# Linear attention and two feed-forward layers on one core: additions moved from GpSimd to VectorE, token quarters loaded singly, order laid anew

## The chip, the core and the metric

The kernel runs on one core of a Trainium2 chip. The metric is device microseconds of one execution, the median of several runs. The core has TensorE (PE, matmuls into PSUM), VectorE (DVE), ScalarE (ACT), GpSimd (POOL), and SyncE (SP), whose queue issues nearly all DMAs. PEld is TensorE's weight load. Each engine works through its own queue in order, with semaphores between them.

## What is computed

Attention with positive features over 4 batches of 8 heads, 576 tokens, head size 64; then two feed-forward layers over the 2304 tokens of width 512, with 2048 inner features.

```python
def _attn_ref(q, k, v, w_phi):
    def phi(x):
        proj = np.einsum('bhsd,df->bhsf', x, w_phi)
        proj = proj - np.max(np.abs(proj), axis=-1, keepdims=True)
        return np.concatenate([np.exp(proj), np.exp(-proj)], axis=-1)
    q_p, k_p = (phi(q), phi(k))
    kv = np.einsum('bhsf,bhsd->bhfd', k_p, v)
    z = np.sum(k_p, axis=2)
    num = np.einsum('bhsf,bhfd->bhsd', q_p, kv)
    den = np.einsum('bhsf,bhf->bhs', q_p, z)[..., None] + 1e-06
    return (num / den).astype(np.float32)
# layer 1: h = x @ w_in; g = h / (1 + exp(-h)); x = g @ w_out
# layer 2: h = max(x @ w_in, 0); out = (h * h) @ w_out
```

## The kernel before

Matmuls of the layers keep nearly full float32 precision: every operand is split into a high part (a cast on ScalarE, `hi_act`, L495) and a low part (source minus high part, `lo_on`, L499), and a product is three matmuls.

The work runs in this order. In **attention**, two heads (a pair) make a unit. `keys_of` (L810) makes the feature sums of keys and values. `queries_of` (L963) takes half of a batch's 576 tokens twice: projection (L1001, L1002), copy out of PSUM on ScalarE (L1016), the largest magnitude over the 128 features, which lie on partitions, by `partition_all_reduce` on GpSimd (L1023), its subtraction on VectorE (L1029), two exponents on ScalarE (L1042), splits, products with the key sums (L1076), and a division through a round trip to HBM. GpSimd also writes ones into the value tiles by memsets (L831, L833).

Interleaved with it, **layer 1 for the first 1280 tokens** runs in plain form: four token blocks of 288, 288, 352 and 352 by 16 chunks of inner features (`chunk`, L1144; products L1161 and L1200). Weights come as 64-bit words and are converted (`w_conv`). `w1_store` (L657) adds each chunk's high and low parts together again and stores the result, for the next part; it makes two additions of 128x512 for each of 16 chunks.

**Layer 1 for the other 1024 tokens, and layer 2**, use a seven-product scheme (Strassen-Winograd) on 2x2 blocks, which needs sums of weight blocks and of token blocks. `w_sums` (L729) loads four 128x256 quarters, splits three of them, makes four sums in place (`w_adds`, L714) and splits those; there are eight pairs of chunks `q` in each of the layers A, B (layer 1, first and second matrix), C and D (layer 2), 32 sets in all. `y_ahead` (L761) does the same earlier for five sets of B and D and parks the result in HBM through the three shared `raw` buffers. `x_sums` (L1227) loads four quarters of a token block, makes four sums and seven splits: once for layer 1 (on VectorE), three times for layer 2. `quad` (L1310) makes the seven products of a first matrix (L1333), combining PSUM banks on VectorE (L1349). `fold` (L1397) loads the activations, makes sums (L1425, L1428, L1431), splits, and the products of a second matrix (L1478).

Order and buffers come from a planner in the kernel (`Plan`): every operation has an engine, an assumed cost, a key (due time) made from the table `KEYS` (L354), and the buffers it holds. At each point an engine takes the ready operation of lowest key, and the instructions are emitted in the order of these starts. Costs and keys thus decide the order in each engine's queue, but nothing on the chip is timed by them. A waiting instruction holds up everything behind it in its queue. A `fixed` buffer is a set place in memory, a `homed` one the next free buffer of a pool.

Of the kernel before, what the change touches and what calls it, by code (L numbers as in the profile page):

```python
# [54 lines left out]
XOWN = {0: (("g0", 0), ("g1", 0), ("g2", 0), ("fs", 0)), 1: (None, None, None, ("x0", 6144))}  # L55
# [291 lines left out]
def dma(kb):  # L347
# [18 lines left out]
def attention_then_two_mlps(ctx, tc, kT, qT, v, w_phi, w1, w2, out):  # L366
# [362 lines left out]
    def w_sums(layer, q, key):  # L729
# [26 lines left out]
        op(key, "POOL", 3700, lambda: w_adds(f), r=[(W, "lo", 0), (W, "lo", 1)], w=[(W, 1)], bufs=[f], unit=u)  # L756
# [4 lines left out]
    def y_ahead(layer, q, key):  # L761
# [5 lines left out]
        def piece(name, a, b, o, r):  # L767
            t = homed("raw", (128, 2, b - a, 256), F32R)
# [18 lines left out]
        gate = [(("ya", layer, AHEAD[layer][k - 1]), "d", "d")] if k else []  # L787
# [3 lines left out]
        op(key, "POOL", 3700, lambda: w_adds(f), r=[(Y, "a"), (Y, "b")], w=[(Y, 1)], bufs=[f], unit=u)  # L791
# [18 lines left out]
    def keys_of(j, p, key):  # L810
# [136 lines left out]
        op(key, "PE", 450, kv_end, r=[(K, "kv", 0), (K, "kv", 1), *done[2]], w=[(K, "t")], bufs=[ps, kv, vt, both], unit=u)  # L947
# [15 lines left out]
    def queries_of(b, p, key, lo_engine="DVE"):  # L963
# [97 lines left out]
        for a in range(2):  # L1061
# [22 lines left out]
            op(key, "PE", 970 if whole else 6 * MM, num_mm, r=[(K, "kvl"), (Q, el, 0), (Q, el, 1)], w=[(Q, "n", a)],  # L1084
# [142 lines left out]
    def x_sums(m, s, key):  # L1227
# [16 lines left out]
        keep = own if alone else own + new  # L1244
# [15 lines left out]
        op(key - 6, "SP", dma(4 * qb), load, r=deps, w=[(X, "raw")], bufs=own)  # L1260

        def split(prod, src, r, key=key, keep=keep):
# [10 lines left out]
            op(key, "ACT", act(2 * qb), hi, r=r, w=[(X, "hi", prod)], bufs=[*keep, b], unit=u)  # L1273
            op(key, "DVE", dve(2 * qb), lo, r=[*r, (X, "hi", prod)], w=[(X, "lo", prod)], bufs=[*keep, b], unit=u)
# [5 lines left out]
        def add(out, x, y, r, name):  # L1280
            e = "DVE" if m == 1 else "POOL"
# [12 lines left out]
        add(t1, b12, b11, first + after(1), "t1")
        add(t3, b22, b12, first + [(X, "t1")], "t3")
        add(t2, b22, t1, [(X, "t1"), (X, "t3")] + after(3), "t2")
        add(t4, b21, t2, [(X, "t2")] + after(2), "t4")
        split(6, t2, [(X, "t2")])
# [98 lines left out]
    def fold(m, i, q, key):  # L1397
# [9 lines left out]
        at_f = None if m == 1 and k < 3 else FOLD[m]["f"][k % 3]  # L1407
# [27 lines left out]
        def split(name, a, b, r):  # L1435
# [3 lines left out]
            engine = "POOL" if m == 1 and name == "a" else "DVE"  # L1439
# [178 lines left out]
    for k, q in enumerate(AHEAD["D"]):  # L1618
        at = base2 + NQ * step * P["ya"] + P["yb"] * k
# [85 lines left out]
```

## Time and profile before

| | us |
|---|---|
| median of 3 runs | 1054.42 |
| lowest, highest | 1051.50, 1059.72 |
| the profiled execution | 1062.31 |
| its span, first to last instruction | 1060.4 |

| engine | busy us | share of the span |
|---|---|---|
| TensorE matmul | 954.4 | 90% |
| VectorE | 762.2 | 72% |
| ScalarE | 610.6 | 58% |
| GpSimd | 278.0 | 26% |

The mean granted clock of TensorE is 0.956 of full speed. A share is an average over stretches with different limits: attention and plain layer 1 until about 519 us, products of `quad` for layer 1 until 590, `fold` until 704, `quad` for layer 2 until 871, and its `fold` to the end. A busy time of TensorE is modelled and is longer at the lower clock. In a table of groups, what follows the bar is busy time, the mean of one, then the idle time of the engine just before them with what ended it ("<-"). "issue" is time in which an engine waited for nothing that the profile shows.

### The profile page before, as it was taken

Reading aid. Unit: us, or ns where it says so; the run is one execution under the profiler, and the core shown is the slowest. Engines: PE = TensorE matmul, PEld = TensorE weight load, DVE = VectorE, ACT = ScalarE, POOL = GpSimd, SP = SyncE. Lnnn points to the kernel's source line nnn. Section 1 sums busy time; section 2 is a strip of 40 time slices with the busy share of each in tenths; the row PEclk is TensorE's granted clock in tenths of the full one; section 3 lists DMA queues with packets and bytes.
Section 4 is the critical chain, followed back from the end, with each engine's and each line's share of the span. In section 5 each row is a group of like instructions: output and inputs, shape, how many; then the busy total and the mean of one; then the engine's idle time right before and its main releaser. Section 6 shows DMA issues by size and latency. Waiting matters only on the chain.

```text
span 1060.4 us, 17832 instructions
## 1 busy us (share of the span) xinstructions
PE 954.4 (90%) x6454; PEld 899.9 (85%) x6454; DVE 762.2 (72%) x1251; ACT 610.6 (58%) x1298; POOL 278.0 (26%) x276
## 2 busy tenths in 40 slices
PE   8889999997676867898899969989999999999998
PEld 7579898897576867788788859989999999999998
DVE  6778988674476454775966799996766678988852
ACT  7777877784354564763654544456656565444431
POOL 2400221102344332343243272463230123000000
PEclk9899999998888978899999989999999999999999
DMA  7689758883466657568456854346463666545422
GB/s 227 216 270 334 258 164 252 267 283 137 152 214 198 216 170 229 173 190 249 139 218 229 277 200 146 114 150 235 150 241 126 234 239 226 162 123 154 140 80 81
DMA packets 103289, 208.45 MB, mean 197 GB/s; under 512 B 16288, under 2 KB 48416, under 8 KB 98080
## 3 DMA queue, kind: packets, MB, share of 16 engines
q1 hardware_dynamic: 103056, 207.23, 59.9%
q8 instruction: 51, 0.84, 0.3%
q14 instruction: 38, 0.31, 0.1%
q10 hardware_dynamic: 144, 0.07, 0.0%
HBM read 136.07 MB, written 71.11 MB: 195 GB/s over the span
## 4 chain that ended last, share of the span: by engine, by line
PE 43%; DVE 11%; issue 4%; DMA 3%; ACT 2%; POOL 2%; SPq 0%; DVEq 0%; POOLq 0%; ACTq 0%
PE y L1478 16%; PE pb L1333 10%; PE pc L1333 6%; PE pa L1333 6%; DVE RA L499 3%; PE h L1161 2%; PE o L1200 2%; DVE x L499 1%; DVE b_w L499 1%; DMA rd<-rr 1%; POOL b_raw L716 1%; DMA b_t<-rd 1%; PE pn L1076 1%; DVE FA L1425 1%; POOL b_t L1023 1%
## 5 line engine op out<-in xcount | busy, mean ns | idle before, releaser
L716 POOL TENSOR_TENSOR b_raw<-b_raw 128x256 f32<-128x256 f32 x128 | 114.6, 898 | 215.3 <-DVE b_w L499 57.9
L495 ACT CAST RA<-x 128x512 fp32r<-128x512 f32 (+2 forms) x146 | 82.4, 587 | 92.2 <-PE y L1478 51.7
L1478 PE MATMUL y<-RA,b_w 128*128 128x256 f32 x912 | 127.0, 281 | 1.6 <-DVE RA L499 1.1
L1478 PEld LDWEIGHTS y<-RA,b_w 128*128 128x128 f32 x912 | 115.7, 189 | 2.4 <-DVE RA L499 1.7
L499 DVE TENSOR_TENSOR RA<-x,RA 128x512 fp32r<-128x512 f32 (+2 forms) x146 | 92.4, 649 | 30.6 <-ACT RA L495 29.9
L1023 POOL PARTITION_ALL_REDUCE b_t<-b_t x28 | 63.2, 2284 | 159.2 <-ACT b_t L1016 66.6
L1478 PE MATMUL y<-RA,b_wq 128*128 128x256 f32 x600 | 90.5, 284 | 5.3 <-DVE RA L499 2.9
L1478 PEld LDWEIGHTS y<-RA,b_wq 128*128 128x128 f32 x600 | 81.9, 192 | 6.5 <-DVE RA L499 3.7
L1200 PE MATMUL o<-b_g,b_w 128*128 128x288 f32 (+1 forms) x420 | 76.6, 326 | 2.5 <-DVE b_g L499 2.5
L1029 DVE TENSOR_TENSOR b_t<-b_t,b_t 128x576 f32<-128x576 f32 x28 | 29.5, 1054 | 65.0 <-POOL b_t L1023 64.9
L1076 PE MATMUL pn<-b_t,b_kv 128*65 128x288 f32 x320 | 58.1, 330 | 18.4 <-ACT b_t L495 6.6
L1200 PE MATMUL o<-b_g,b_wq 128*128 128x352 f32 (+1 forms) x348 | 65.3, 329 | 8.7 <-DVE b_g L499 5.9
L1042 ACT ACTIVATE b_t<-b_t 128x576 f32<-128x576 f32 x56 | 37.7, 681 | 59.2 <-DVE b_t L1029 52.6
L1200 PEld LDWEIGHTS o<-b_g,b_w 128*128 128x128 f32 x420 | 67.1, 201 | 3.8 <-DVE b_g L499 3.5
L1161 PE MATMUL h<-b_x,b_w 128*128 128x288 f32 (+1 forms) x420 | 69.2, 315 | 1.1 <-DVE FA L1169 1.1
L1076 PEld LDWEIGHTS pn<-b_t,b_kv 128*65 128x65 f32 x320 | 43.5, 146 | 30.1 <-DVE b_kv L940 6.9
L1333 PE MATMUL pb<-RA,b_w 128*128 128x384 f32 (+1 forms) x312 | 68.8, 350 | 0.0
L1161 PEld LDWEIGHTS h<-b_x,b_w 128*128 128x128 f32 x420 | 64.9, 195 | 1.6 <-DVE FA L1169 1.4
L1200 PEld LDWEIGHTS o<-b_g,b_wq 128*128 128x128 f32 x348 | 56.5, 199 | 11.1 <-DVE b_g L499 7.0
L499 DVE TENSOR_TENSOR b_t<-b_t,b_t 128x576 fp32r<-128x576 f32 (+1 forms) x72 | 55.6, 780 | 12.0 <-ACT b_t L495 10.4
L1161 PE MATMUL h<-b_x,b_wq 128*128 128x352 f32 (+1 forms) x348 | 58.5, 319 | 1.8 <-DVE FA L1169 0.9
L499 DVE TENSOR_TENSOR b_w<-b_raw,b_w 128x1024 fp32r<-128x1024 f32 (+2 forms) x59 | 54.8, 939 | 6.6 <-ACT b_w L495 5.2
(188 smaller groups left out, 2243.0 us busy)
## 6 DMA issues: line engine op xcount, KB each, us to landing
b_wq<-w1d SPq DMA_DIRECT2D x18, 1024.0 KB, 7.2
b_raw<-w SPq DMA_DIRECT2D x32, 512.0 KB, 5.9
x<-gd SPq DMA_DIRECT2D x32, 512.0 KB, 3.7
gd<-g SPq DMA_DIRECT2D x36, 384.0 KB, 2.4
b_w<-w SPq DMA_DIRECT2D x11, 1024.0 KB, 7.5
w2d<-FA SPq DMA_DIRECT2D x32, 256.0 KB, 4.4
w1f<-b_raw SPq DMA_DIRECT2D x16, 512.0 KB, 3.2
b_raw<-w1f SPq DMA_DIRECT2D x32, 256.0 KB, 4.1
```

The source lines that it names most:

```text
L495: nc.scalar.copy(out=dst, in_=src)
L499: e.tensor_tensor(out=dst, in0=src, in1=hi.bitcast(F32), op=ALU.subtract)
L716: nc.gpsimd.tensor_tensor(out=get(f)[:, o], in0=get(f)[:, a], in1=get(f)[:, b], op=how)
L1023: nc.gpsimd.partition_all_reduce(get(mx), get(pr).rearrange("p a t -> p (a t)"), 128, bass.bass_isa.ReduceOp.absmax)
L1029: nc.vector.tensor_tensor(out=f, in0=f, in1=get(mx), op=ALU.subtract)
L1042: nc.scalar.activation(out=flat(e), in_=f, func=AF.Exp, scale=1.0 - 2.0 * s)
L1076: nc.tensor.matmul(get(ps)[:D1, :HB], w, flat(e)[:, t], start=x == 0, stop=x == len(ops) - 1)
L1161: nc.tensor.matmul(get(ps)[:, :cols], a, x[:, cc, :cols], start=k == 0, stop=k == 3 * ND - 1)
L1200: nc.tensor.matmul(get(acc)[:, :cols], a, g, start=c == 0 and x == 0, stop=c == NC - 1 and x == 2)
L1333: nc.tensor.matmul(get(ps)[:, :qb], ws[a][:, f], get(b)[:, y, cc], start=first and k == 0, stop=k == 5, skip_group_check=True,)
L1425: nc.vector.tensor_tensor(out=part(0, 2), in0=get(f)[:, 1:4:2, :half], in1=part(0, 2), op=ALU.subtract)
L1478: nc.tensor.matmul(get(acc)[:, d * 256:d * 256 + half], get(ws[a][0])[:, ws[a][1], s], both(y)[:, j], start=q == 0 and d == 0 and x == 0, ...
```

## The change

All four kinds of additions that GpSimd made go to VectorE: the four sums of a weight set (`w_adds`), the merges in `w1_store` (one of 128x1024 in place of two of 128x512), the token sums of layer 2 in `x_sums`, and the low part of split "a" in `fold` of layer 1. `x_sums` loads its four quarters as four operations, each with its own dependants and buffers, in place of one. The first inputs of layer 1's `fold` have other homes, as have the fourth quarter of layer 2's first token block and the pieces of `y_ahead` for D, which waits for the first product of layer 2. Some of the planner's costs change by a little, and the keys nearly all change.

```diff
-XOWN = {0: (("g0", 0), ("g1", 0), ("g2", 0), ("fs", 0)), 1: (None, None, None, ("x0", 6144))}
+XOWN = {0: (("g0", 0), ("g1", 0), ("g2", 0), None), 1: (None, None, None, ("x0", 6144))}
@@ FOLD
-    1: {"f": (("FA", 0), ("FA", 4096), None), ...
+    1: {"f": (("fs", 0), ("FA", 0), ("FA", 4096)), ...
@@ KEYS (the part that is named below; nearly all others change too)
-    "ss": 35.86, "wa": -0.61, "wb": 4.29, "wc": 32.0, "ba": 46.13, "bb": 9.59, "x1": 32.79, "x2": 28.35, "xe":
+    174.03, "ss": -10.38, "wa": -1.73, "wb": 9.37, "wc": 3.99, "ba": 32.07, "bb": 33.22, "x1": 114.67, "x2":
+    -3.46, "xe": 17.39, "mg": 6.56, "md": 524, "mp": 304, "me": 50,
@@ w1_store
-        def merge(x):
-            nc.gpsimd.tensor_tensor(out=get(f)[:, x], in0=halves(0)[:, x], in1=halves(1)[:, x], op=ALU.add)
+        def merge():
+            nc.vector.tensor_tensor(out=get(f), in0=halves(0), in1=halves(1), op=ALU.add)
...
-        u = plan.unit()
-        for x in range(2):
-            op(key, "POOL", pool(512), lambda x=x: merge(x), r=r + [(("c", 0, i, c), "h")], w=[("wm", c, x)], bufs=[w, f], unit=u)
-        op(key, "SP", dma(512), store, r=[("wm", c, x) for x in range(2)], w=[(("wf", 0, c), "d")], bufs=[f])
+        op(key, "DVE", dve(1024), merge, r=r + [(("c", 0, i, c), "h")], w=[("wm", c)], bufs=[w, f], unit=plan.unit())
+        op(key, "SP", dma(512), store, r=[("wm", c)], w=[(("wf", 0, c), "d")], bufs=[f])
@@ w_adds
-            nc.gpsimd.tensor_tensor(out=get(f)[:, o], in0=get(f)[:, a], in1=get(f)[:, b], op=how)
+            nc.vector.tensor_tensor(out=get(f)[:, o], in0=get(f)[:, a], in1=get(f)[:, b], op=how)
@@ w_sums
-        op(key, "POOL", 3700, lambda: w_adds(f), r=[(W, "lo", 0), (W, "lo", 1)], w=[(W, 1)], bufs=[f], unit=u)
+        op(key, "DVE", 4 * dve(256), lambda: w_adds(f), r=[(W, "lo", 0), (W, "lo", 1)], w=[(W, 1)], bufs=[f], unit=u)
@@ y_ahead
-            t = homed("raw", (128, 2, b - a, 256), F32R)
+            shape = (128, 2, b - a, 256)
+            t = homed("raw", shape, F32R) if layer == "B" else fixed(("RA", 43008 if b - a == 2 else 47104), shape, F32R)
...
-        gate = [(("ya", layer, AHEAD[layer][k - 1]), "d", "d")] if k else []
+        gate = [(("ya", layer, AHEAD[layer][k - 1]), "d", "d")] if k else [(("q", 2, 0, 0), "p1")] if layer == "D" else []
...
-        op(key, "POOL", 3700, lambda: w_adds(f), r=[(Y, "a"), (Y, "b")], w=[(Y, 1)], bufs=[f], unit=u)
+        op(key, "DVE", 4 * dve(256), lambda: w_adds(f), r=[(Y, "a"), (Y, "b")], w=[(Y, 1)], bufs=[f], unit=u)
@@ x_sums
-        def load():
-            for i in range(2):
-                for j in range(2):
-                    at = (2 * s + j) * qb
-                    nc.sync.dma_start(out=raw(i, j if i == 0 else 1 - j), in_=(x1d if m == 1 else x2d)[:, 2 * i:2 * i + 2, at:at + qb])
+        def load(i, j):
+            at = (2 * s + (j if i == 0 else 1 - j)) * qb
+            nc.sync.dma_start(out=raw(i, j), in_=(x1d if m == 1 else x2d)[:, 2 * i:2 * i + 2, at:at + qb])
...
-        op(key - 6, "SP", dma(4 * qb), load, r=deps, w=[(X, "raw")], bufs=own)
+        for i, j in ((0, 0), (0, 1), (1, 0), (1, 1)):
+            op(key - 6, "SP", dma(qb), lambda i=i, j=j: load(i, j), r=deps, w=[(X, "raw", i, j)], bufs=[ob(i, j)])
...
-        def add(out, x, y, r, name):
-            e = "DVE" if m == 1 else "POOL"
+        def add(out, x, y, r, name, keep):
+            e = "DVE"
@@ fold
-        at_f = None if m == 1 and k < 3 else FOLD[m]["f"][k % 3]
+        at_f = FOLD[m]["f"][k % 3] if m == 2 or k not in (1, 2) else None
...
-            engine = "POOL" if m == 1 and name == "a" else "DVE"
+            engine = "DVE"
```

## Rows read from the trace of the kernel before

**Rows 1.** Busy time by stretch: from:to, length, engines (instructions), clock, DMA share, GB/s.

```profile
75.00:219.00 144.00, 135.34 (x1045) 130.33 (x1044) 115.62 (x208) 112.38 (x267) 23.28 (x25) 0.99 0.83 263
219.00:460.00 241.00, 184.52 (x1193) 175.07 (x1193) 136.82 (x226) 131.47 (x343) 78.94 (x66) 0.87 0.60 192
460.00:519.00 59.00, 51.63 (x293) 47.77 (x292) 43.27 (x65) 32.22 (x60) 17.72 (x21) 0.97 0.75 226
...
590.00:704.00 114.00, 96.74 (x728) 91.86 (x726) 104.44 (x145) 55.31 (x99) 57.76 (x51) 0.96 0.55 180
704.00:871.00 167.00, 166.56 (x952) 166.18 (x953) 114.39 (x191) 104.29 (x205) 43.51 (x40) 1.00 0.56 200
```

**Rows 2.** Waits, 219 to 519 us: who waited for whom, us, times, longest.

```profile
DVE b_t L1029 <- POOL b_t L1023: 62.9, 9, 11.2
POOL b_t L1023 <- issue: 50.1, 7, 9.6
ACT b_t L1042 <- DVE b_t L1029: 49.9, 8, 10.9
```

**Rows 3.** Instructions of L1023, L663 and L716: count, ns min/median/max, first and last start.

```profile
L1023 POOLq MODIFY_POOL_CONFIG  x18: 1/11/40, 245.9 to 446.8; - x18
...
L663 POOLq MODIFY_POOL_CONFIG  x16: 87/98/98, 219.5 to 408.1; - x16
...
L716 POOLq MODIFY_POOL_CONFIG  x4: 4/46/88, 434.8 to 460.8; - x4
```

**Rows 4.** Timeline of GpSimd, 110 to 135 us: start, us, instruction, idle before.

```profile
121.62 2.14 POOL L1023 PARTITION_ALL_REDUCE b_t<-b_t  x1 [5.05 <-ACT b_t L1016]
```

**Rows 5.** Timeline of all engines, 251 to 258 us.

```profile
252.18 2.16 POOL L1023 PARTITION_ALL_REDUCE b_t<-b_t  x1 [6.45 <-issue]
254.37 0.76 DVE L1029 TENSOR_TENSOR b_t<-b_t,b_t 128x576 f32<-128x576 f32 x1 [7.63 <-POOL b_t L1023]
...
255.22 0.68 ACT L1042 ACTIVATE b_t<-b_t 128x576 f32<-128x576 f32 x1 [7.11 <-DVE b_t L1029]
...
256.24 0.61 PE L1001 MATMUL pq<-b_t,wst_lo 128*128 128x288 f32 x1 [6.67 <-ACT b_t L1016]
```

**Rows 6.** Timeline of TensorE, 219 to 470 us: the last of eight stalls.

```profile
429.73 2.71 PE L1200 MATMUL o<-b_g,b_wq 128*128 128x352 f32 x8 [4.86 <-DVE b_g L499]
```

**Rows 7.** VectorE by form, whole span: the L1115 and L1284 groups.

```profile
L1115 DVE TENSOR_TENSOR b_xx<-b_t,b_t 64x288 f32<-64x288 f32 x56 | 31.5, 563 | 7.5 <-DMA b_t<-rd 6.9
...
L1284 DVE TENSOR_TENSOR b_wl<-b_wl,b_wl 128x1024 f32<-128x1024 f32 x2 | 2.4, 1217 | 0.0
```

**Rows 8.** VectorE by form, 900 to 1050 us.

```profile
L499 DVE TENSOR_TENSOR RA<-x,RA 128x512 fp32r<-128x512 f32 x86 | 58.0, 687 | 29.2 <-ACT RA L495 28.8
...
L1428 DVE TENSOR_TENSOR x<-x 128x256 f32<-128x256 f32 x26 | 10.9, 419 | 0.1
```

**Rows 9.** VectorE by form, 590 to 704 us: first and last of 19 forms.

```profile
L499 DVE TENSOR_TENSOR x<-FA,x 128x512 fp32r<-128x512 f32 x17 | 16.7, 987 | 0.3 <-ACT x L495 0.2
...
L499 DVE TENSOR_TENSOR b_wl<-b_raw,b_wq 128x256 fp32r<-128x256 f32 x2 | 1.4, 682 | 0.0
```

**Rows 10.** GpSimd by form in 75 to 219, 219 to 460 and 590 to 704 us.

```profile
L1023 POOL PARTITION_ALL_REDUCE b_t<-b_t x10 | 22.7, 2293 | 80.3 <-ACT b_t L1016 42.8 <-DMA b_v<-v 19.9 <-issue 9.1
...
L1023 POOL PARTITION_ALL_REDUCE b_t<-b_t x15 | 32.4, 2182 | 77.5 <-issue 50.1 <-ACT b_t L1016 13.2 <-DMA rd<-rr 8.3
...
L716 POOL TENSOR_TENSOR b_raw<-b_raw 128x256 f32<-128x256 f32 x32 | 31.4, 982 | 16.5 <-DVE b_w L499 7.5 <-DMA b_w<-ysdB 4.5 <-DVE b_wl L499 2.2
```

**Rows 11.** Chain that ended last, 860 to 900 us: start, us, what.

```profile
883.16 2.69 POOL b_raw L716
...
887.89 0.75 POOL b_raw L716
```

**Rows 12.** Waits of GpSimd, 590 to 900 us.

```profile
POOL b_raw L716 <- DMA gd<-g: 46.3, 1, 46.3
...
POOL x L1284 <- DMA b_raw<-x2d: 25.9, 3, 13.1
```

More of the change, by code (lines that the diff above doesn't have):

```diff
@@ L860, in keys_of @@
         both = slot(f"kd{n}_2", u, (128, 2, F))
-        op(key, "PE", NKT * 218 + 140, proj, r=[(K, "raw"), "wraw"], w=[((K, a), "p") for a in range(2)],
+        op(key, "PE", NKT * 218 + 220, proj, r=[(K, "raw"), "wraw"], w=[((K, a), "p") for a in range(2)],
            bufs=[raw, *pk[:2], *mxs[:2]], unit=u)
-        op(key, "PE", 218, proj_end, r=[(K, "end"), "wraw", ((K, 0), "p")], w=[((K, 2), "p")], bufs=[end, pk[2], mxs[2]], unit=u)
+        op(key, "PE", 140, proj_end, r=[(K, "end"), "wraw", ((K, 0), "p")], w=[((K, 2), "p")], bufs=[end, pk[2], mxs[2]], unit=u)
         for g in range(3):
@@ L1009, in queries_of @@
         if whole:
-            op(key - (P["p1"] if b == 1 else 0), "PE", 4 * 120 + 140, proj_rows, r=[(Q, "raw"), "wraw"],
+            op(key - (P["p1"] if b == 1 else 0), "PE", 4 * 120 + 210, proj_rows, r=[(Q, "raw"), "wraw"],
                w=[(Q, "p", a) for a in range(2)], bufs=[raw, *pqs, pr], unit=u)
@@ L1083, in queries_of @@
             el = "e" if whole else "el"
-            op(key, "PE", 970 if whole else 6 * MM, num_mm, r=[(K, "kvl"), (Q, el, 0), (Q, el, 1)], w=[(Q, "n", a)],
+            op(key, "PE", 990 if whole else 6 * MM + 6, num_mm, r=[(K, "kvl"), (Q, el, 0), (Q, el, 1)], w=[(Q, "n", a)],
                bufs=[kv, ps, num] + [x for hl_ in hls for x in hl_], unit=u)
@@ L1243, in x_sums @@
             fresh = lambda i, j: get(new[2 * i + j])
-        keep = own if alone else own + new
-        def load():
-            for i in range(2):
-                for j in range(2):
-                    at = (2 * s + j) * qb
-                    nc.sync.dma_start(out=raw(i, j if i == 0 else 1 - j), in_=(x1d if m == 1 else x2d)[:, 2 * i:2 * i + 2, at:at + qb])
+        ob = lambda i, j: own[i] if m == 1 else own[2 * i + j]
+        nb = ob if alone else lambda i, j: new[2 * i + j]
+        def load(i, j):
+            at = (2 * s + (j if i == 0 else 1 - j)) * qb
+            nc.sync.dma_start(out=raw(i, j), in_=(x1d if m == 1 else x2d)[:, 2 * i:2 * i + 2, at:at + qb])
         if m == 1:
@@ L1259, in x_sums, with split @@
         turn = [(("xr", m, s - 1), "lo", prod) for prod in SLOT] if s else []
-        op(key - 6, "SP", dma(4 * qb), load, r=deps, w=[(X, "raw")], bufs=own)
-        def split(prod, src, r, key=key, keep=keep):
+        for i, j in ((0, 0), (0, 1), (1, 0), (1, 1)):
+            op(key - 6, "SP", dma(qb), lambda i=i, j=j: load(i, j), r=deps, w=[(X, "raw", i, j)], bufs=[ob(i, j)])
+        def split(prod, src, r, keep, key=key):
             b = fixed(XT[m][prod], (128, 2, 2, qb), F32R)
@@ L1272, in split @@
             r = [*r, *turn]
-            op(key, "ACT", act(2 * qb), hi, r=r, w=[(X, "hi", prod)], bufs=[*keep, b], unit=u)
-            op(key, "DVE", dve(2 * qb), lo, r=[*r, (X, "hi", prod)], w=[(X, "lo", prod)], bufs=[*keep, b], unit=u)
+            op(key, "ACT", act(2 * qb), hi, r=r, w=[(X, "hi", prod)], bufs=[keep, b], unit=u)
+            op(key, "DVE", dve(2 * qb), lo, r=[*r, (X, "hi", prod)], w=[(X, "lo", prod)], bufs=[keep, b], unit=u)
         b11, b12 = (lambda: raw(0, 0)), (lambda: raw(0, 1))
@@ L1288, in x_sums @@
-        first = [(X, "raw")]
+            op(key - 1, e, dve(2 * qb) if e == "DVE" else pool(2 * qb), go, r=r, w=[(X, name)], bufs=list(dict.fromkeys(keep)), unit=u)
+        r11, r12, r22, r21 = ((X, "raw", i, j) for i, j in ((0, 0), (0, 1), (1, 0), (1, 1)))
         after = (lambda *ps: [(X, "lo", p) for p in ps]) if alone else (lambda *ps: [])
-        split(1, b11, first)
+        split(1, b11, [r11], ob(0, 0))
         if alone:
-            split(2, b21, first)
-            split(3, b22, first)
@@ L1294, in x_sums @@
[L1294 to L1298, printed above, removed]
+            split(2, b21, [r21], ob(1, 1))
+            split(3, b22, [r22], ob(1, 0))
+        add(t1, b12, b11, [r11, r12] + after(1), "t1", [ob(0, 1), ob(0, 0), nb(0, 0)])
+        add(t3, b22, b12, [r12, r22, (X, "t1")], "t3", [ob(1, 0), ob(0, 1), nb(0, 1)])
@@ L1299, in x_sums @@
+        add(t2, b22, t1, [r22, (X, "t1"), (X, "t3")] + after(3), "t2", [ob(1, 0), nb(0, 0), nb(1, 0)])
+        add(t4, b21, t2, [r21, (X, "t2")] + after(2), "t4", [ob(1, 1), nb(1, 0), nb(1, 1)])
+        split(6, t2, [(X, "t2")], nb(1, 0))
         if not alone:
-            split(2, b21, first)
-        split(7, t3, [(X, "t3")])
-        split(5, t1, [(X, "t1")] + ([(X, "t2")] if alone else []))
+            split(2, b21, [r21], ob(1, 1))
+        split(7, t3, [(X, "t3")], nb(0, 1))
+        split(5, t1, [(X, "t1")] + ([(X, "t2")] if alone else []), nb(0, 0))
@@ L1303, in x_sums @@
         if not alone:
-            split(3, b22, first)
+            split(3, b22, [r22], ob(1, 0))
         if m == 2 and s == 0:
-            later.append(lambda key: split(4, t4, [(X, "t4")], key, own[3:]))
+            later.append(lambda key: split(4, t4, [(X, "t4")], nb(1, 1), key))
         else:
-            split(4, t4, [(X, "t4")])
+            split(4, t4, [(X, "t4")], nb(1, 1))
     def quad(m, s, q, key):
```

7 lines of the change are left out of this document (3 added, 4 removed), and 13 rows, old and new, of tables (FOLD, KEYS).

## The prediction

> **What bounds the kernel now.** The table by stretches comes first. From 704 to 871 us TensorE is busy 166.56 of 167 us and nothing is to be had there [rows 1]. Two long stretches are not full. In 219 to 460 TensorE idles 241 - 184.52 = 56.5 us and its granted clock is 0.87; in 75 to 219, the same mix of attention and first-layer chunks, it idles 8.7 of 144 at 0.99 [rows 1]. In 590 to 704 TensorE has 96.74 of 114, while VectorE has 104.44 of 114: VectorE bounds that stretch [rows 1].
>
> Then the waits of 219 to 519. The longest is a chain: VectorE's subtraction (L1029) waited 62.9 us for GpSimd's partition reduction (L1023), ScalarE's exponent (L1042) 49.9 us for that subtraction, and the reduction itself 50.1 us for "issue", that is for nothing the profile shows [rows 2]. The reader should ask what GpSimd does in those 50 us. The instructions of the lines tell: 18 MODIFY_POOL_CONFIG ahead of reductions, 16 ahead of the merges (L663), 4 ahead of the sums of weights (L716), all between 219.5 and 460.8 us [rows 3]. They come in twos, so GpSimd changes between the reduction and plain additions 19 times here. At 121.62 us, where only reductions and memsets stand in its queue, a reduction follows its ScalarE copy without such a gap [rows 4].
>
> One change, followed through the engines: the reduction starts at 252.18 after 6.45 us of "issue"; VectorE had stood 7.63 us, ScalarE 7.11 us, TensorE 6.67 us [rows 5]. ScalarE works in order, so its blocked exponent holds up the copy from PSUM (L1016) behind it, which TensorE's row names. The TensorE timeline of 219 to 460 has eight stalls over 4.8 us, each beside a late reduction: 6.67, 7.18, 6.64, 5.65, 5.47, 6.19, 4.98, 4.86, together 47.6 us (the first in [rows 5], the last in [rows 6]). The other idle time of the stretch is 8.9 us.
>
> **The change part by part.** *GpSimd loses every addition.* It keeps reductions and memsets, the mixture of before 219 us, which needed no MODIFY_POOL_CONFIG [rows 3, 4]. So I expect all 19 changes to go. The gain is at least nothing, if the query blocks are paced by something else, and at most all 47.6 us. Six stalls end at the query chain or an instruction right behind it, 36.6 us, and I count them whole; the two that end at L893 (6.19) and at a chunk's split (4.86) have other parents too, and I count half, 5.5. Term: -42.1. What is late next: an idle share like that of 75 to 219 (6%) on the some 193 us that remain is 11.6 us against 8.9 now: +2.7.
>
> The clock: a mean of 0.87 is 26% of 241 us, 63 us, at 1.2 instead of 2.4 GHz [rows 1]. If the 47.6 us of stalls lie in it, 15 us of work ran slow; at full clock this takes half, a gain of 0 to 8 us. I take -4.
>
> *The 32 half merges (L663) become 16 of 128x1024 on VectorE*, 1217 ns each undisturbed [rows 7]: 19.5 us, and four sums of weights (419 ns [rows 8]) 1.7 us, in a stretch where VectorE is busy 136.82 of 241 [rows 1]. Against it stands relief: VectorE's additions are slower while GpSimd adds. In 590 to 704 17 splits of 128x512 took 987 ns, where one took 687 in 900 to 1050, with GpSimd idle [rows 8, 9]. Over the 19 forms of that stretch that are above their undisturbed time (the first and the last in [rows 9]) this excess is 21.8 us, for 58 us of GpSimd's time [rows 1], 0.38 us per us. In 219 to 460 GpSimd works 78.9 us, 32.4 of them on reductions [rows 1, 10]; the other 46.5 give a relief of 18, so +3 net. I put all 3 on the path, since the query chain passes VectorE; without relief it would be +21.
>
> *Sums of weights (L716), 32 sets of four.* In 460 to 519 GpSimd works 17.7 us, 18 additions at the 982 ns of [rows 10]: 7.5 us on VectorE less a relief of 6.7; I take +2, because VectorE feeds the first product there. In 590 to 704: 32 sums (13.4 us), the fold's 16 splits (6.7 us) and four sums of 128x768 tokens (0.95 us, between the 687 of 512 and the 1217 of 1024; 3.8 us) are added, 23.9 us, against 21.8 of relief: +2.1 where VectorE bounds [rows 1, 7, 8, 9, 10]. On the other side each set of four leaves GpSimd's 982 ns for 419, and the later due times of the third layer's sums (key wc 32 to 4, x2 28 to -3) let some wait until after 704, where VectorE has 114.39 of 167. Bounds -16 (four sets of 4 us: four sums and the splits of 256, 512 and 1024) to +23.9; I take -2 in all. In 871 to 897 four sums hold the chain from 883.16 on, the first 2.69 us [rows 11]; they end by 888.6, and four of 419 ns take 1.7 instead of 5.5. Bounds -4 to 0; I take -2.
>
> *Tokens of the third layer.* The eight sums of its second and third blocks (7.6 us) lie in 704 to 871, beside full TensorE work, with 52 us of VectorE free: 0 while no one waits. Loading the quarters one by one issues the same four transfers on SP; an early quarter can start earlier. The fold's other homes and y_ahead's fixed ones leave the three shared buffers freer; the gate added there is the first product after 704, with the rest of that stretch still ahead. 0 each, bounds -3 to +3. If the cover in 704 to 871 were gone, the eight sums would cost 7.6.
>
> *The order.* The new keys move almost every due time, at the start too. I cannot price it by rows: 0, with -8 to +8 for 0 to 75 us, where nothing else changes.
>
> Sum: -42.1 + 2.7 - 4 + 3 + 2 - 2 - 2 = -42.4. The profiled execution took 1062.31 us (span 1060.4), 7.9 above the median of 1054.42; I carry the difference over: 1054.4 - 42.4 = **1012 us**.
>
> **The rivals.** *A. VectorE pays in full.* Relief does not come, because VectorE's slower additions have some other cause. Then 590 to 704 costs 21.8 more, 1034 us. For it: VectorE is busy 92% there. Against: one form of one size differs by 300 ns between a stretch with GpSimd and one without [rows 8, 9]. The Trainium skill (Perfetto Trace Analysis, Optimizing Scalar/DVE Operations) speaks against this change: a saturated VectorE may be unloaded onto GpSimd, and this does the reverse; by it alone the kernel would go to this rival's time. The same section warns that the two share a read port and such a move might not help; the trace agrees with the warning, 987 against 687 ns. Chance 0.14.
>
> *B. The switches were not the pace.* From 75 to 219 ten reductions run, 14 us apart; from 219 to 460 fifteen (one of them begun before), 16 us apart [rows 10]: hardly slower. So blocks may be paced by buffers or by the order, and late reductions only fill slack. Then -42.1, +2.7 and -4 vanish: 1054.4 + 1 = 1055 us, no change. Against: the eight stalls begin where ScalarE stands behind the late reduction [rows 5], and from 75 to 219 TensorE was full, so that pace was TensorE's. Chance 0.13.
>
> *C. Slower: the moved additions wait in VectorE's queue.* GpSimd stood waiting for transfers at no price: 25.9 us for tokens (L1284) and 46.3 us once before sums of weights [rows 12], 72.2 together. VectorE works in order, and behind such a wait stand the sums that free TensorE's PSUM banks, mostly in 704 to 871 where TensorE has no slack. In full this would be 1012 + 72.2 = 1084; it undoes the gain from 42 us on, and slows by over 1% from 53 us. Against: the planner starts an instruction only when it counts its transfer as landed, and the multiplications behind transfers (L1115, 56 of them) cost VectorE 7.5 us of idle time in all [rows 7]. Chance 0.12.
>
> **How the numbers follow.** The forecast (992 to 1030 by the bounds of its terms) has 0.58, A 0.14, B 0.13, C 0.12, and 0.03 stays for a gain beyond 62 us. About 1% is what a measurement of this kernel can tell from no change (1044 to 1065). Faster: 0.58 + 0.14 + 0.03 = 0.75; same 0.13; slower 0.12. The range goes from 988, which leaves out 0.03, to 1060, which leaves out C and a little of B, 0.15.
>
> **What would show it.** Right: MODIFY_POOL_CONFIG only at the start; the reduction within 0.3 us of its copy; L1029's wait for L1023 down from 62.9 to under 15 us; the stretch that was 219 to 460 near 200 us at a clock over 0.95; VectorE's splits of 128x512 all near 690 ns, its total near 800 us. Wrong: VectorE waiting for transfers ahead of L716, L1284 or L663; the fold's stretch 20 us longer; TensorE stalls of 5 us in attention with no late reduction beside them.

## The result, and the profile after

The changed kernel takes 967.19 us (median; 966.76 to 967.53) against 1054.01 us before: a ratio of 0.9169, 95% interval 0.9132 to 0.9207. The direction was forecast, the size was not: -87 us where -42 was expected, and outside the range.

Where the time went is read by stages. The table gives, from the traces, when TensorE starts the first product of layer 1's `quad`, and then the length of each stage (up to the first product of the next). By this measure the kernel before reaches its stages at 510.4, 590.2, 694.1 and 871.4 us; the prediction cut its stretches at 519 and 704, so the last 10 us of its stretch for the fold belong to the next stage. The rows below the second are the experiments, told further down.

| us | attention and plain layer 1, to | quad, layer 1 | fold, layer 1 | quad, layer 2 | last fold | span |
|---|---|---|---|---|---|---|
| before | 510.4 | 79.8 | 103.9 | 177.3 | 189.0 | 1060.4 |
| after | 441.0 | 78.8 | 83.3 | 175.1 | 186.8 | 965.0 |
| b_merge | 445.8 | 78.6 | 104.4 | 176.6 | 183.1 | 988.5 |
| a_merge_pool | 487.6 | 78.7 | 83.4 | 175.0 | 181.0 | 1005.7 |
| b_merge_tiny | 478.7 | 79.5 | 104.2 | 178.2 | 190.4 | 1031.0 |
| a_tiny16 | 449.4 | 78.8 | 84.9 | 175.8 | 188.4 | 977.3 |
| a_tiny4 | 446.9 | 77.7 | 84.9 | 175.9 | 188.4 | 973.8 |
| b_all | 441.7 | 82.8 | 96.5 | 182.5 | 181.8 | 985.3 |
| a_adds_pool | 448.7 | 83.2 | 88.4 | 179.6 | 184.6 | 984.5 |
| b_newkeys | 530.3 | 84.8 | 96.0 | 186.1 | 188.9 | 1086.1 |
| a_oldkeys | 434.3 | 87.2 | 87.5 | 178.3 | 187.1 | 974.4 |
| b_planned | 446.3 | 82.5 | 120.1 | 184.1 | 186.8 | 1019.8 |
| b_planned_homes | 454.9 | 82.1 | 98.0 | 188.5 | 181.0 | 1004.5 |
| a_oneload | 441.1 | 79.9 | 90.5 | 182.8 | 186.8 | 981.1 |

Two stages carry the gain: attention with -69 and the fold of layer 1 with -21; the others give 1 to 2 us each. (These are the profiled executions; that of before took 8 us more than its median.)

The page of the kernel after, busy time and share by engine:

```profile
PE 928.6 (96%) x6494; PEld 881.4 (91%) x6494; DVE 791.1 (82%) x1423; ACT 610.9 (63%) x1298; POOL 78.7 (8%) x88
```

Busy time by stretch, kernel after (columns as in [rows 1]); the stretches from 441 on are its stages:

```profile
219.00:400.00 181.00, 173.54 (x1240) 166.24 (x1239) 144.59 (x256) 135.01 (x352) 32.99 (x32) 1.00 0.86 270
441.00:520.00 79.00, 76.80 (x328) 60.77 (x327) 74.03 (x127) 46.16 (x77) 0.00 (x0) 1.00 0.57 198
520.00:603.00 83.00, 81.64 (x683) 80.38 (x682) 79.39 (x148) 44.72 (x80) 0.00 (x0) 1.00 0.61 200
603.00:778.00 175.00, 174.50 (x999) 173.45 (x998) 142.64 (x271) 113.72 (x221) 0.00 (x0) 1.00 0.63 218
```

Before, 1193 matmuls filled the 241 us from 219 on, with 56.5 us of idle time and a clock of 0.87 [rows 1]. Now 1240 fit in 181 us, with 7.5 idle at 1.00. In the fold, TensorE idles 1.4 us. VectorE, 96% busy there, is now the engine with the least room beside TensorE.

The reduction's line, kernel after, whole span: what GpSimd's idle time ahead of it ended on, and who waited for it (us, times):

```profile
its engine sat idle before it (us, times) until:
  ACT b_t L1015: 144.4, 15
  issue: 32.6, 2
...
who waited for it (us, times):
  DVE b_t L1028: 8.6, 6
```

VectorE's wait for the reduction fell from 62.9 us [rows 2] to 8.6 over the whole span. There is no MODIFY_POOL_CONFIG after the first microseconds, against 38 between 219 and 461 us [rows 3]. Two idle times of GpSimd are still put down to "issue", without any such instruction and with no one waiting for them: a long "issue" row alone is no sign of a change. (Here and below a *change* is a switch of GpSimd between the reduction and additions; the traces show each as two MODIFY_POOL_CONFIG.)

VectorE by form, kernel after, 520 to 603 us:

```profile
L499 DVE TENSOR_TENSOR x<-FA,x 128x512 fp32r<-128x512 f32 x16 | 10.8, 684 | 0.0
...
L714 DVE TENSOR_TENSOR b_raw<-b_raw 128x256 f32<-128x256 f32 x12 | 5.1, 425 | 0.4
```

The split that took 987 ns beside GpSimd's additions [rows 9] takes 684. And only 12 sums of weights lie in this stage, where GpSimd made 24 in it before (the 32 of [rows 10] reach 10 us into the next stage). GpSimd by form, kernel before, 590 to 694 us:

```profile
L716 POOL TENSOR_TENSOR b_raw<-b_raw 128x256 f32<-128x256 f32 x24 | 23.6, 982 | 15.7 <-DVE b_w L499 7.1 <-DMA b_w<-ysdB 4.5 <-DVE b_wl L499 2.2
```

### The profile page after: what moved, and what is told of

Read it like the earlier page. It is cut to its first block, busy times and chain, and to the rows that moved or that the text cites. A ratio compares the mean times of both kernels' runs of the same rounds, so it can differ in the third digit from the quotient of the medians.

```text
span 965.0 us, 17716 instructions
## 1 busy us (share of the span) xinstructions
PE 928.6 (96%) x6494; PEld 881.4 (91%) x6494; DVE 791.1 (82%) x1423; ACT 610.9 (63%) x1298; POOL 78.7 (8%) x88
## 4 chain that ended last, share of the span: by engine, by line
PE 42%; DVE 16%; DMA 2%; issue 2%; ACT 1%; SPq 0%; DVEq 0%; ACTq 0%
PE y L1477 18%; PE pb L1332 8%; PE pc L1332 5%; PE pa L1332 5%; DVE RA L499 3%; DVE b_raw L714 2%; PE o L1199 2%; PE h L1160 2%; DVE x L499 2%; DVE b_w L499 2%; DVE g L1348 1%; DMA b_t<-rd 1%; DVE FA L1348 1%; DVE b_wq L499 1%; DMA b_raw<-w 1%
## 5 line engine op out<-in xcount | busy, mean ns | idle before, releaser
L495 ACT CAST RA<-x 128x512 fp32r<-128x512 f32 (+2 forms) x146 | 82.7, 588 | 90.0 <-PE y L1477 46.6
L1199 PE MATMUL o<-b_g,b_w 128*128 128x288 f32 (+1 forms) x420 | 72.2, 312 | 0.2 <-DVE b_g L499 0.2
L1199 PE MATMUL o<-b_g,b_wq 128*128 128x352 f32 (+1 forms) x348 | 61.1, 315 | 3.5 <-ACT b_g L495 2.5
L1199 PEld LDWEIGHTS o<-b_g,b_w 128*128 128x128 f32 x420 | 62.5, 188 | 1.7 <-DVE b_g L499 0.5
L1332 PEld LDWEIGHTS pb<-RA,b_w 128*128 128x128 f32 x312 | 55.9, 188 | 4.8 <-DVE fs L1348 0.8
L499 DVE TENSOR_TENSOR b_w<-b_raw,b_w 128x1024 fp32r<-128x1024 f32 (+2 forms) x59 | 49.8, 856 | 12.6 <-ACT b_w L495 10.3
L495 ACT CAST b_w<-b_raw 128x1024 fp32r<-128x1024 f32 (+2 forms) x59 | 43.9, 756 | 24.5 <-DVE b_raw L714 20.7
L1075 PE MATMUL pn<-b_t,b_kv 128*65 128x288 f32 x320 | 54.1, 314 | 5.0 <-ACT b_t L1078 2.2
L495 ACT CAST b_t<-b_t 128x576 fp32r<-128x576 f32 x72 | 48.0, 674 | 15.1 <-DMA b_t<-qT 11.0
L1199 PEld LDWEIGHTS o<-b_g,b_wq 128*128 128x128 f32 x348 | 53.0, 188 | 4.9 <-ACT b_g L495 3.1
L714 DVE TENSOR_TENSOR b_raw<-b_raw 128x256 f32<-128x256 f32 x128 | 54.3, 424 | 3.8
```

The lines of the kernel that those rows point to most:

```text
L495: nc.scalar.copy(out=dst, in_=src)
L499: e.tensor_tensor(out=dst, in0=src, in1=hi.bitcast(F32), op=ALU.subtract)
L714: nc.vector.tensor_tensor(out=get(f)[:, o], in0=get(f)[:, a], in1=get(f)[:, b], op=how)
L1075: nc.tensor.matmul(get(ps)[:D1, :HB], w, flat(e)[:, t], start=x == 0, stop=x == len(ops) - 1)
L1199: nc.tensor.matmul(get(acc)[:, :cols], a, g, start=c == 0 and x == 0, stop=c == NC - 1 and x == 2)
L1332: nc.tensor.matmul(get(ps)[:, :qb], ws[a][:, f], get(b)[:, y, cc], start=first and k == 0, stop=k == 5, skip_group_check=True,)
```

## The experiments

Labels that begin with b_ start from the kernel before, those with a_ from the kernel after. "Order untouched" means that the plan still counts the operation on its old engine and only the engine that issues it differs, so each queue keeps its order. A ratio is to the kernel before as measured beside the run; its medians there are 1053.75, 1058.07 and 1054.78 us, so times in us carry a few us of this. The stages are from one execution of each kernel.

### What the merges alone are worth

**b_merge**, before with the 32 half merges on VectorE, order untouched:

```diff
-            nc.gpsimd.tensor_tensor(out=get(f)[:, x], in0=halves(0)[:, x], in1=halves(1)[:, x], op=ALU.add)
+            nc.vector.tensor_tensor(out=get(f)[:, x], in0=halves(0)[:, x], in1=halves(1)[:, x], op=ALU.add)
```

> The kernel before, with its order untouched: the planner still plans the 32 merges as GpSimd work, and only the instruction is put on VectorE at the same place of the order. Theory S (GpSimd's changes between reduction and additions set the pace of 219 to 460 us): 15 or 16 of the 19 changes go, the stretch shortens by 40 us or more, about 1005 to 1015 us. Theory O (the gain beyond that comes from the new order): with the old order little is won, within 15 us of 1054. Both: a few MODIFY_POOL_CONFIG remain at the sums of weights after 430 us.

Measured 989.98 us, ratio 0.9408 (0.9355 to 0.9461), 15 us below what Theory S expected. One word of the source brings 64 of the 87 us. The kernel b_merge, busy time by stretch:

```profile
219.00:395.00 176.00, 166.38 (x1176) 159.27 (x1175) 141.17 (x255) 130.33 (x341) 33.26 (x33) 0.99 0.81 260
...
524.00:629.00 105.00, 89.43 (x689) 85.14 (x688) 94.23 (x132) 50.56 (x94) 53.23 (x43) 0.95 0.56 181
```

Its merges on VectorE by form, 219 to 445 us:

```profile
L663 DVE TENSOR_TENSOR b_raw<-b_w 128x512 f32<-128x512 f32 x16 | 11.0, 685 | 0.8 <-DMA w1f<-b_raw 0.7
L663 DVE TENSOR_TENSOR b_raw<-b_wq 128x512 f32<-128x512 f32 x16 | 10.8, 686 | 0.1
```

The configuration instructions that are left after the start, by line, as in [rows 3]:

```profile
L1023 POOLq MODIFY_POOL_CONFIG  x2: 11/11/11, 384.7 to 384.7; - x2
L716 POOLq MODIFY_POOL_CONFIG  x4: 4/46/88, 371.6 to 398.0; - x4
```

The longest wait of 219 to 500 us:

```profile
POOL b_t L1023 <- ACT b_t L1016: 70.5, 10, 23.9
```

The order is the same, so the first stretch compares directly with the second row of [rows 1]. Idle time of TensorE: 56.5 to 9.6, -46.9. Busy time: -18.1, of which 17 matmuls fewer are 2.4 (at 141 ns); the other 15.7 us go with the clock, 0.87 to 0.99. The whole of attention, before and then b_merge, tells the same:

```profile
0.00:510.40 510.40, 429.27 (x2903) 396.45 (x2903) 342.02 (x571) 326.14 (x773) 141.31 (x144) 0.92 0.69 220
```

```profile
0.00:445.80 445.80, 413.97 (x2902) 384.49 (x2903) 348.97 (x603) 326.39 (x773) 98.72 (x112) 0.98 0.78 252
```

TensorE idles 49 us less and is busy 15 us less with the same matmuls. VectorE's busy time rose by 7.0 us although it took over 21.8 us of merges; its other instructions became some 15 us shorter. 16 of the 19 changes are gone. VectorE waited 0.7 us for transfers ahead of the merges.

**a_merge_pool**, after with the merges on GpSimd again, as two halves, order untouched:

```diff
-            nc.vector.tensor_tensor(out=get(f), in0=halves(0), in1=halves(1), op=ALU.add)
+            for x in range(2):
+                nc.gpsimd.tensor_tensor(out=get(f)[:, x], in0=halves(0)[:, x], in1=halves(1)[:, x], op=ALU.add)
```

> The changed kernel with the merges issued on GpSimd again, 32 of 128x512 at the places where the planner had VectorE's; the order is the new one. Theory S': the price of a change is what the order leaves between a reduction's due time and the end of its code's loading. With tiny additions that wait for nothing the new order paid 13 us for six changes back. Real merges wait for their data and so change later: 985 to 1030 us. If the loading alone counted, 980.

Measured 1011.46 us (0.9597, 0.9560 to 0.9633), 44 us over after, all of it in attention (487.6 for 441.0; its last fold is 6 us shorter, see the last section). The waits of 219 to 500 us in a_merge_pool are those of [rows 2] again:

```profile
DVE b_t L1029 <- POOL b_t L1023: 46.5, 8, 11.6
ACT b_t L1042 <- DVE b_t L1029: 44.8, 8, 9.1
POOL b_t L1023 <- issue: 42.4, 6, 10.2
```

The effect is there in both orders. It has 12 changes here: 46.6 / 12 = 3.9 us each, beside (510.4 - 445.8) / 16 = 4.0 in b_merge.

### The change of operation, or the length of the additions?

Both kernels above take away two things, the changes and 1.4 us additions in GpSimd's queue. The next three put the changes back with additions of one partition and 8 numbers, whose result nobody uses.

**b_merge_tiny**, b_merge with such an addition at each half merge, which reads the merge's first numbers and so waits for what the merge waits for:

```diff
+            nc.vector.tensor_tensor(out=get(f)[:, x], in0=halves(0)[:, x], in1=halves(1)[:, x], op=ALU.add)
+            nc.gpsimd.tensor_tensor(out=ticked, in0=halves(0)[:1, x, :8], in1=halves(1)[:1, x, :8], op=ALU.add)
```

> The run with the merges alone on VectorE (990 us), and at each half merge's place in the order one addition of 1x8 on GpSimd that reads the merge's first eight numbers, so that it waits for the same data; nobody uses its result. Theory S: the 19 changes between reduction and additions come back and with them the late reductions, 1035 to 1055 us. Rival R (the long additions' hold on the port, or VectorE's time, made the 64 us): within 10 us of 990.

Measured 1031.96 us (0.9794, 0.9763 to 0.9825), 3 us below Theory S's range and far from the rival's. The waits of 219 to 500 us:

```profile
POOL ticked L666 <- issue: 57.1, 8, 7.7
DVE b_t L1032 <- POOL b_t L1026: 40.3, 6, 10.7
ACT b_t L1045 <- DVE b_t L1032: 38.0, 8, 10.4
```

One of the two groups of little additions, GpSimd by form, 219 to 479 us:

```profile
L666 POOL TENSOR_TENSOR ticked<-b_w 1x8 f32<-1x8 f32 x16 | 5.8, 365 | 30.1 <-issue 29.1
```

An addition of 0.36 us waits 57.1 / 8 = 7.1 us for nothing the profile shows, and the chain of late subtractions and exponents is back. Attention takes 33 us more than in b_merge: half of the 65. This half holds the changes and the waiting for the merges' data in GpSimd's queue, for one transfer 11.6 us; this run does not part them. The other half comes only with the full additions of 1.4 us each (45 us in all). Whether they cost it by standing ahead of reductions or by slowing VectorE is not shown. (The last fold of this kernel is 7 us longer as well; see the last section.)

**a_tiny16** and **a_tiny4**, after with one such addition behind each of the 16 merges, or behind four of them, which waits for nothing:

```diff
             nc.vector.tensor_tensor(out=get(f), in0=halves(0), in1=halves(1), op=ALU.add)
+            if c % 4 == 1:                     # a_tiny16: if True
+                nc.gpsimd.tensor_tensor(out=ticked, in0=tick, in1=tick, op=ALU.add)
```

> The changed kernel with one addition of 1x8 on GpSimd issued behind each of the 16 merges; its result is used by nobody. It moves no VectorE work and keeps no port busy. Theory S (each change from additions back to the reduction delays a due reduction by about 7 us, and the end with it, as the run with the merges alone showed: 64 us for 9 such changes): 967 plus 7 us for each change back to L1022 that the trace shows, 1015 to 1070 us for 7 to 15 of them. Rival R (the gain of the moved merges was the port that GpSimd's long additions held, or VectorE's time): within 10 us of 967.

> The same with a tiny addition behind four of the 16 merges (chunks 1, 5, 9, 13). Theory S: at most four changes back, 975 to 995 us, about a quarter of what 16 cost. Rival R: 967.

Measured 979.07 us (0.9246, 0.9182 to 0.9310) and 971.96 us (0.9192, 0.9136 to 0.9248). Theory S misses both, the first by 36 us; the rival's 10 us miss the first by 2. The longest waits of a_tiny16 in the same stretch:

```profile
POOL ticked L668 <- issue: 54.5, 6, 11.5
...
DVE b_t L1033 <- POOL b_t L1027: 20.3, 7, 5.3
```

12 changes cost attention 8.4 us, 0.7 each, and 6 changes 5.9, 1.0 each; the interval of a_tiny4 still holds after's ratio. So a change has no fixed price. GpSimd stands no shorter for it (54.5 / 6 = 9.1 us, idle time included), but VectorE waits 20.3 us for late reductions instead of 40.3. In b_merge_tiny, in the old order and with the addition waiting for the merge's data, it is 33 / 16 = 2.1 us each; with full additions 4. That the little additions of a_tiny16 fall into time in which no reduction is ready is the likely reason, and argued only.

The Trainium skill (GPSIMD Engine Reference, the section on instruction dispatch) states that a first call to a freshly loaded GpSimd routine pays about 6 us. The trace agrees in size: 6.45 us of "issue" ahead of the first reduction in [rows 5], 7.1 ahead of the little additions.

### The other additions

**b_all**, before with all four kinds issued on VectorE, order untouched (the edits of b_merge and the like in `w_adds`, `x_sums` and `fold`):

> The kernel before, with its order untouched, and all four kinds of additions issued on VectorE at the places where the planner had GpSimd's. Theory S: no MODIFY_POOL_CONFIG after the start, 219 to 460 shortens as in the run with the merges alone or by some us more, and the fold's stretch stays within 5 us of 114 since relief and added work cancel: 995 to 1010 us. Theory O: the fold's stretch and attention stay long, over 1040. Theory C of the prediction (VectorE waits for transfers): over 1054.

Measured 987.92 us (0.9383, 0.9357 to 0.9410), 2 us from b_merge and not to be told from it, and 7 us below Theory S's range, which held the fold's stretch for unchanged. Inside, more moved. Busy time by stretch, b_all:

```profile
524.00:621.00 97.00, 85.30 (x688) 81.73 (x687) 91.58 (x173) 50.47 (x93) 0.00 (x0) 1.00 0.59 196
621.00:803.00 182.00, 175.79 (x996) 173.87 (x995) 137.75 (x254) 109.06 (x211) 0.00 (x0) 0.99 0.54 192
```

The fold is 8 us shorter than in b_merge: VectorE takes over 43 additions (20.3 us by their rows in b_all) and is busy 2.7 us less, so its others gave back 23 us, near the 21.8 that the prediction counted for them. The stage gains more than VectorE's 2.7 us: TensorE idles 4 us less, and its clock of 1.00 for 0.95 goes with 4 us less of busy time. The second quads are 6 us longer, with TensorE idle for 6.2 us instead of 2.6, 5.4 of them behind VectorE's sums of PSUM banks (L1349): additions put there at nothing have a price.

**a_adds_pool**, after with the sums of weights on GpSimd again, order untouched:

```diff
-            nc.vector.tensor_tensor(out=get(f)[:, o], in0=get(f)[:, a], in1=get(f)[:, b], op=how)
+            nc.gpsimd.tensor_tensor(out=get(f)[:, o], in0=get(f)[:, a], in1=get(f)[:, b], op=how)
```

> The changed kernel with the sums of weights issued on GpSimd again, the order untouched. VectorE loses 53 us of additions and its two-input instructions slow down beside GpSimd. If relief and added work cancel, as the prediction held: the fold's stretch within 4 us of 83; the whole 967 to 985 us, the excess from changes of code in the last reductions before 400 us and from GpSimd's longer sets in the chain.

Measured 985.12 us (0.9348, 0.9315 to 0.9382), +18: attention +8 (three changes), the first quads +4, the fold +5, the second quads +5. The fold was expected within 4 us. Three kinds of additions moved together are worth 2 us in the old order; the sums of weights alone are worth 18 in the new one. That it was laid for VectorE's shorter sums is the likely reason, and argued only.

### Order, homes and quarters

**b_newkeys**, before with nothing but the new `KEYS`, and **a_oldkeys**, after with the old ones (the edit is the table in the diff of the change):

> The kernel before with the new keys alone: all additions stay on GpSimd. Theory S: the changes between reductions and additions stay (15 or more), and with them late reductions and stalls: 1030 to 1070 us. Theory O: most of the gain is there, under 1010 us.

> The changed kernel with the table of keys of the kernel before: additions are planned and issued on VectorE, the quarters and homes are the new ones, only the due times are the old. Theory S with little from the order: under 985 us. If the new keys carry the part that was not foreseen (some 45 us): 1000 to 1015 us, with the fold's stretch near 110 us and attention some 20 us longer than in the changed kernel.

Measured 1086.41 us (1.0307, 1.0263 to 1.0350, slower) and 976.15 us (0.9270, 0.9233 to 0.9307). The first is 16 us over Theory S's range, the second as Theory S had it. The new order by itself costs 33 us. By stages it is 20 in attention, 5 and 9 in the quads, and the fold is 8 shorter. For attention the waits of 219 to 500 us in b_newkeys tell:

```profile
DVE b_t L1029 <- POOL b_t L1023: 81.6, 10, 13.7
POOL b_raw L663 <- issue: 53.1, 7, 9.4
POOL b_t L1023 <- issue: 44.7, 6, 10.2
```

It has 21 changes instead of 19, and VectorE waits 81.6 us for late reductions instead of 62.9 [rows 2]. With GpSimd free of additions the same keys gain 9 us.

**b_planned**: before with all additions planned as well as issued on VectorE (the edits of the change in `w1_store`, `w_adds`, `w_sums`, `y_ahead`, `x_sums` and `fold` as far as they name the engine), old keys, homes and loads. **b_planned_homes** adds the homes of the fold's inputs and of the fourth token quarter:

```diff
-XOWN = {0: (("g0", 0), ("g1", 0), ("g2", 0), ("fs", 0)), ...
+XOWN = {0: (("g0", 0), ("g1", 0), ("g2", 0), None), ...
-    1: {"f": (("FA", 0), ("FA", 4096), None), ...
+    1: {"f": (("fs", 0), ("FA", 0), ("FA", 4096)), ...
-        at_f = None if m == 1 and k < 3 else FOLD[m]["f"][k % 3]
+        at_f = FOLD[m]["f"][k % 3] if m == 2 or k not in (1, 2) else None
```

> The kernel before with all additions planned as VectorE work and issued there (one merge of 1024 in place of two), the old keys, homes and loads. Against the run that only issued them there (988 us, fold's stretch 96 us): if the planner's knowing of VectorE's load is what shortened the fold's stretch to 88 us with the old keys, 972 to 982 us. If the quarters or homes did it: 984 to 992.

> The same with the other homes of the fold's first inputs and of the fourth token quarter. If these homes shorten the fold's stretch: 5 us or more below the run without them, near the 976 of the changed kernel with the old keys. If they only make room that nobody needs: within 3 us of it.

Measured 1023.24 us (0.9697, 0.9634 to 0.9759) and 1005.32 us (0.9503, 0.9443 to 0.9564). Neither forecast for b_planned (972 to 992) holds; the homes bring 18 us, but end 29 over the 976 of a_oldkeys. Telling the planner the truth costs 35 us against b_all, 24 of them in the fold (120.1 for 96.5). The timeline of b_planned around its longest stall:

```profile
632.26 0.37 SPq L1418 DMA_DIRECT2D b_raw<-gd  x1
635.80 0.92 ACT L495 CAST x<-b_raw 128x256 fp32r<-128x256 f32 x2 [5.07 <-DMA b_raw<-gd]
636.24 0.42 DVE L499 TENSOR_TENSOR x<-b_raw,x 128x256 fp32r<-128x256 f32 x1 [4.04 <-ACT x L495]
...
636.26 1.90 PE L1476 MATMUL y<-x,b_w 128*128 128x256 f32 x6 [16.22 <-ACT x L495]
```

What the load of the fold's input waited for in SyncE's queue, 610 to 634 us:

```profile
SPq L1418 <- DVE b_w L499: 5.1, 1, 5.1
```

The load is issued at 632.26, into a shared `raw` buffer, once VectorE is done with a split of weights, and TensorE stands 16.22 us until the input has come and is split. With the other homes the fold is 98.0 us. This is the part that the prediction priced at nothing.

**a_oneload**, after with the four token quarters loaded by one operation again:

```diff
-        for i, j in ((0, 0), (0, 1), (1, 0), (1, 1)):
-            op(key - 6, "SP", dma(qb), lambda i=i, j=j: load(i, j), r=deps, w=[(X, "raw", i, j)], bufs=[ob(i, j)])
+        four = ((0, 0), (0, 1), (1, 0), (1, 1))
+        op(key - 6, "SP", dma(4 * qb), lambda: [load(i, j) for i in range(2) for j in ((0, 1) if i == 0 else (1, 0))], r=deps,
+           w=[(X, "raw", i, j) for i, j in four], bufs=list(dict.fromkeys(ob(i, j) for i, j in four)))
```

> The changed kernel with the four token quarters loaded by one operation again. If the quarters carry a part of what the plan with old homes and loads lost: 5 to 25 us over 967, with TensorE or ScalarE waiting for the first x casts before 441 and 603 us. If they carry nothing: within 3 us of 967.

Measured 984.47 us (0.9353, 0.9311 to 0.9395), +17, within what was expected: the fold +7, the second quads +8. Busy time by stretch, a_oneload, beside the rows of after for these two stages:

```profile
521.00:611.00 90.00, 84.68 (x681) 82.81 (x680) 81.81 (x153) 47.12 (x83) 0.00 (x0) 0.96 0.56 183
611.00:794.00 183.00, 176.28 (x1001) 173.66 (x1000) 140.72 (x266) 113.08 (x217) 0.00 (x0) 1.00 0.60 209
```

TensorE idles 5.3 and 6.7 us there instead of 1.4 and 0.5, while no engine is fuller.

One way down the whole change, by medians: before 1054; merges issued on VectorE 990; the other additions too 988; the same planned as such 1023; the fold's homes 1005; quarters, the homes of `y_ahead` and small costs 976 (not taken apart on this side; quarters alone are 17 from the other side); the new keys 967. The steps do not add up in another sequence, as b_newkeys and a_adds_pool show. No kernel tried is faster than after.

## Why the prediction was right or wrong

**The bottleneck and its cause: right.** GpSimd's changes between reductions and additions set the pace of attention. b_merge and a_merge_pool give the size of the merges on GpSimd, changes and additions together; in the old order the little additions alone bring half of it back. Rival B (the changes are not the pace) is refuted by b_merge.

**The stalls: right, a little small.** Expected -42.1 + 2.7 = -39.4 us of idle time for 219 to 460; b_merge shows -46.9. The halves that were cut from two stalls were there to be had, and the idle time left over did not grow with the mixture of 75 to 219 but stayed at 9.6.

**The clock: the term that was mis-sized most in attention.** I took -4 and called 0 to -8 its bounds; the rows give -15.7. The step that failed is "if the 47.6 us of stalls lie in it, 15 us of work ran slow". The 63 us at 1.2 GHz do not cover the stalls; half of them (twice 15.7) lie over work. Two neighbouring stretches of the kernel before, which the prediction didn't look at, would have told; below them, 24 products of one line and shape in each:

```profile
320.00:340.00 20.00, 12.42 (x66) 11.75 (x65) 11.35 (x16) 9.37 (x28) 8.88 (x9) 0.74 0.54 169
340.00:360.00 20.00, 19.28 (x143) 18.49 (x142) 10.67 (x19) 13.08 (x41) 7.37 (x9) 1.00 0.98 333
```

```profile
L1200 PE MATMUL o<-b_g,b_wq 128*128 128x352 f32 x24 | 5.7, 394 | 0.0
```

```profile
L1200 PE MATMUL o<-b_g,b_wq 128*128 128x352 f32 x24 | 4.6, 327 | 0.0
```

Busy time per matmul is 188 ns at 0.74 and 135 at 1.00, but the mix differs; the 24 products take 5.7 us in the first and 4.6 in the second. In this stage a stall is paid twice, once as idle time and again as slow work.

**The merges on VectorE: relief right, price wrong.** The relief was put at 18 and came as 15 (b_merge). But the +3 that I put on the path cost nothing that can be seen. Attention as a whole: -40.4 forecast, -64.6 in b_merge.

**The other additions: right in sum by luck, wrong in place.** +2, -2 and -2 were forecast for them, and b_all shows -2 in total, but as -8 in the fold (+2.1 without the later due times), +4 in the first quads (forecast +2), +6 in the second (forecast 0, or 7.6 if the cover was gone) and -1 to -4 elsewhere. In the fold 23.9 us of added work was too much: 8 of the 32 sums lie behind the stage, and GpSimd made 15 splits in it, not 16; 20.3 us came. And no term stood there for the clock, 0.95 before, which goes with half of the 8 us. Rival A (VectorE pays in full) falls: the relief in the fold is 23 us by b_all, and the split takes 684 ns for 987 in after. The advice of the Trainium skill to unload a saturated VectorE onto GpSimd (Perfetto Trace Analysis, Optimizing Scalar/DVE Operations) would have gone the wrong way here. Its warning that the two share a read port, so that such a move might not help, agrees with the rows, 987 for 684 ns; that the port is the cause is not shown.

**Homes, quarters, order at 0: wrong, and the second large miss.** They were bounded by -3 to +3 and -8 to +8. Measured: homes -18 (after planning on VectorE), quarters -17, keys +33 without the rest and -9 with it. The step that failed is "0 each": a shared buffer that comes free late stops TensorE for 16 us. Planning on VectorE, which I took as free, costs 35 us until homes and quarters take it back. Together they end 21 us below b_all, mostly in the fold (96.5 to 83.3), where VectorE has 25 instructions fewer: 173 in b_all, 172 in b_planned_homes, 158 in a_oldkeys, 148 in after, by the same view. By the rows, three sets of weights (24 sums to 12) and 12 us of VectorE's work left the stage, where my bound of -16 allowed four sets. So the work that I let leave only as a bound did leave, and not by the due times alone. My low bounds together come to -79 us, or 975; the range began at 988, and 967 lies below both.

**Rival C (waits for transfers in VectorE's queue): not seen.** In after VectorE waits for transfers 1.9 us ahead of the merges and 0.7 ahead of the token sums, and at no sum of weights.

In short, by the profiled executions, against which the sum was made (-95.4 us where -42.4 was forecast):

| us | forecast | measured |
|---|---|---|
| attention (idle, clock, merges) | -40.4 | -69.4 |
| first quads | +2 | -1.0 |
| fold of layer 1 | -2 | -20.6 |
| second quads and last fold | -2 | -4.4 |

The +2 was for 460 to 519 us, most of which lies ahead of the first quads. By medians the gain is 87: 8 us are that the profiled execution of before was a long one, and which stage held them is not shown.

## What to carry to other kernels

If two kinds of operation on GpSimd bring a MODIFY_POOL_CONFIG at each change between them, give it one kind only; the price of a change is not its 6 to 7 us but what waits behind it, here 0.7 to 2.1 us each with little additions, and 4 with the full ones. Price a stall with the slow work after it: take busy time per matmul in stretches at both clock levels. And an order is part of the placement it was laid for: test the keys alone and the placement alone before either is called free.

## What the runs showed of the hardware

The last fold came in different lengths with the same products. Busy time by stretch, 115 us near the end, of after and then of b_merge:

```profile
845.00:960.00 115.00, 115.00 (x979) 115.00 (x978) 79.13 (x146) 43.41 (x77) 0.00 (x0) 1.00 0.39 115
```

```profile
868.00:983.00 115.00, 115.00 (x1017) 115.00 (x1017) 83.23 (x154) 45.36 (x82) 0.00 (x0) 1.00 0.41 120
```

TensorE is full and at a clock of 1.00 in both, yet a matmul of 256 columns follows the last after 117.5 ns in one and 113.1 in the other: some 6 us of the stage. Before, a_oldkeys, b_newkeys, b_planned and a_oneload are like after; b_all, b_planned_homes, a_merge_pool and a_adds_pool like b_merge; the three kernels with little additions are a little slower than after (972 matmuls in 115 us of a_tiny16, 118.3 ns each). More than one kind ran on one chip in one series. Between before and b_merge the edit leaves TensorE's own instructions and addresses as they are, so the cause lies elsewhere. Only one execution of each kernel was traced, so it could also change from one execution to the next. It stays open, and 6 of the 64 us of b_merge may be its.
